# K and V of an attention kernel read as rows of two keys, two partial row sums, and a third tile in every fourth head on TensorE

## The chip, the cores and the metric

The kernel runs on one core of one Trainium2 chip. The metric is the device time of one execution in microseconds. Before the change it is 1547.74 us, the median of three runs (1547.68 to 1548.92). One more execution was taken with the hardware profiler; the views in this document are from that one.

## What is computed

A block of a transformer with adaptive normalization. The heavy part is attention of 2048 queries over a cache of 2048 keys, 32 heads of 128, in bf16:

```python
h = _layernorm(x, axis=-1) * (1 + ca) + sa
q = (h @ wq).reshape(B, Sq, 32, 128).transpose(0, 2, 1, 3)
scores = jnp.einsum('bhqd,bhkd->bhqk', q, k_cache) * 128 ** (-0.5)
p = _softmax(scores, axis=-1)
o = jnp.einsum('bhqk,bhkd->bhqd', p, v_cache)
x = x + ga * (o.transpose(0, 2, 1, 3).reshape(B, Sq, 4096) @ wo)
```

After it come a second normalization and a mixer with an MLP on the 2048 x 640 activations. The change does not touch them.

## The kernel before

Every engine has one list of instructions, written out in program order by the functions `op` and `dma`, which also work out the semaphore waits from the keys that an instruction reads and writes. Nothing reorders a list later: an instruction that waits holds up all that stands behind it on its engine. SyncE (SP) issues nearly all transfers, so its list is also the order in which they enter the DMA queue q1. GpSimd (POOL) issues the stores of the attention output into a scratch tensor in memory, `o_scratch` (line 477).

The attention loop (line 560) runs over 512 steps, 32 heads of 16 query tiles of 128 queries. In step s:

- TensorE multiplies the query tile with all 2048 keys of the head, in two halves of two 512-column matmuls each (`qk`, lines 299 and 15), into `Sps`. Between the halves and behind them stand the halves of the P V product of the step eight back (`pv`, line 313; `PVD` is 8), and the small pieces below.
- VectorE scales each half by the negative factor, writes it to `negS` in SBUF and takes the row minimum (line 606). GpSimd joins the two minima (line 611). ScalarE takes the exponential into a slot of a ring of ten, `Pb` (line 614).
- The exponentials have queries on the partitions, and P V needs keys there, so each tile is transposed. Most tiles go by DMA within SBUF (`transpose`, line 233), two neighbouring tiles in one transfer where possible. Some are done by TensorE in float32 pairs of bf16 values (`t_piece`, line 265: eight 128x128 transposes a tile, spread over two steps), and ScalarE copies them out of PSUM (`t_evac`, line 272: two copies of 512 columns a tile). `PE_STEPS` has two patterns: kind 0 gives TensorE the tiles 3 and 10 of a head, kind 1 the tiles 2, 3 and 10; each number behind a tile is the step at which its pieces begin. `kind(h)` is `h % 2`, so heads have two and three such tiles in turn.
- In the first kind the DMA transposes 14 tiles of a head in eight transfers, six pairs and two singles (tiles 2 and 11); in the second 13 tiles in seven, six pairs and a single (tile 11).
- The queries of the next head are made in 20 pieces of one 512-column matmul (`q_piece`, line 248) with four copies on ScalarE (line 255), placed where no transpose piece stands.

`pv` multiplies 16 blocks of 128 keys with `Vaug`, whose blocks have 130 columns: 128 of V and a one, so that the 129th result is the row sum of the exponentials. Two query tiles share a PSUM bank; ScalarE copies both, 259 columns, to `Of` (line 593). For every four tiles GpSimd raises the four row sums to the power of -1 (`rcp`, line 463), multiplies (`norm`, line 470) and stores.

The loads of a head come on SyncE between the transposes: at step 2 K of the next head (`load_k`, line 216, a transposing DMA of 2048 rows of 128), at step 6 the weights of the queries (`load_wq`, line 220), at step 9 V of the next head (`load_v`, line 225: 16 blocks of 128 keys, 256 bytes a key). K, V and wq have two buffers each.

The ones beside V are written once at the start: GpSimd fills a scratch area, TensorE transposes it, ScalarE copies it, GpSimd copies a part of it into `Vaug` (lines 357 to 365).

Behind the loop the kernel loads the attention output transposed from memory (`load_ot`, line 520; the first parts already within the last head) and runs the output projection (line 548) and the rest.

Of the kernel before, what the change touches and what calls it, by code (L numbers as in the profile page):

```python
# [9 lines left out]
F32 = mybir.dt.float32  # L10
# [113 lines left out]
def bass_adaLN_cond__mha_block_cached__mixer_s_mlp__prompt_kernel(  # L124
# [6 lines left out]
    KT = D // 128  # L131
# [14 lines left out]
    with ExitStack() as es:  # L146
# [9 lines left out]
        if True:  # L156
            with ExitStack() as es1:
# [3 lines left out]
                PE_STEPS = ({3: 6, 10: 13}, {2: 5, 3: 7, 10: 14})  # L161
                kind = lambda h: h % 2
                US = KT * (SQ + 4)
# [18 lines left out]
                KTs = kv[:, 0:o1].rearrange("p (b s) -> p b s", b=2)  # L182
                Vaug = kv[:, o1:o2].rearrange("p (b k d) -> p b k d", b=2, k=NKT)
                wq = kv[:, o2:o3].rearrange("p (b k d) -> p b k d", b=2, k=KT)
# [29 lines left out]
                def load_k(h):  # L214
                    hb = h % 2
                    G.dma("sync", lambda e: e.dma_start_transpose(KTs[:, hb], A_k_cache[0, h]), ("k", hb), w=[("KT", hb)])

# [5 lines left out]
                def load_v(h):  # L223
                    hb = h % 2
                    G.dma("sync", lambda e: e.dma_start(Vaug[:, hb, :, 0:128], A_v_cache[0, h].rearrange("(t p) d -> p t d", p=128)),
                          ("v", hb), w=[("V", hb)])
# [78 lines left out]
                def pv(g, half):  # L305
                    hb = (g // NQT) % 2
                    b = g % RP
                    ob = PO[:, ((g // 2) % 2) * 512 + (g % 2) * 130:]

                    def f(t):  # L310
                        for kt in range(half * 8, half * 8 + 8):
                            pt = PTr[:, b, kt // 2, :, kt % 2] if is_pe(g) else PTs[:, b, kt, :]
                            ins = t.matmul(ob[:, 0:129], pt, Vaug[:, hb, kt, 0:129],  # L313
                                           start=(kt == 0), stop=(kt == NKT - 1))
                        return ins
                    G.op("tensor", f, r=[("PT", b, half), ("V", hb), "ones"], w=[("O", (g // 2) % 2)])

# [28 lines left out]
                if H > 1:  # L346
# [9 lines left out]
                G.op("gpsimd", lambda g: g.tensor_copy(identf[:], ident), r=["ident"] + ringk(IO, IO + 128), w=["identf"])  # L356
                half1 = flat[:, 0:256].rearrange("p (q z) -> p q z", z=2)
                G.op("gpsimd", lambda g: g.memset(half1, 0.0), w=["h0", ("Pb", 0)])
                G.op("gpsimd", lambda g: g.memset(half1[:, :, 0], 1.0), r=["h0"], w=["h1"])
                G.op("tensor", lambda t: t.transpose(JB[0][:, 0:128], flat[:, 0:256].bitcast(F32), identf[:]),  # L360
                     r=["h1", "identf"], w=[("J", 0)])
                G.op("scalar", lambda a: a.copy(flat[:, 256:512].bitcast(F32), JB[0][:, 0:128]), r=[("J", 0)], w=["h2"])
                G.op("gpsimd", lambda g: g.tensor_copy(
                    Vaug[:, :, :, 128:130], flat[:, 256:384].rearrange("p (b k y z) -> p b k y z", b=2, k=NKT, z=2)[:, :, :, :, 0]),
                    r=["h2", ("Pb", 0)], w=["ones"])
                G.op("scalar", lambda a: a.activation(s_col, c_sb, ACT.Silu), r=["c"], w=["scol"])
# [94 lines left out]
                def rcp(gr):  # L461
                    b = gr % 2
                    G.op("gpsimd", lambda g: g.tensor_tensor(  # L463
                        out=rl[:, 4 * b:4 * b + 4], in0=Of[:].rearrange("p a z d -> p (a z) d")[:, 4 * b:4 * b + 4, 128],
                        in1=mone, op=ALU.pow),
                         r=[("Of", 2 * b), ("Of", 2 * b + 1), "mone"], w=[("rl", b)])

                def norm(gr, z):
                    b = gr % 2
                    G.op("gpsimd", lambda g: g.tensor_scalar(  # L470
                        out=On[:, b, z, :], in0=Of[:, 2 * b + z // 2, z % 2, 0:128],
                        scalar1=rl[:, 4 * b + z:4 * b + z + 1], scalar2=1.0, op0=ALU.mult, op1=ALU.mult),
                        r=[("Of", 2 * b + z // 2), ("rl", b)], w=[("On", b, z)])
                    if z < 3:
                        return
                    hh, jj = divmod(4 * gr, NQT)
                    G.dma("gpsimd", lambda e: e.dma_start(  # L477
                        o_scr[jj // 2:jj // 2 + 2, :, hh].rearrange("a p z d -> p a (z d)"),
                        On[:, b].rearrange("p (a z) d -> p a (z d)", a=2)),
                        ("o", b), r=[("On", b, z) for z in range(4)], w=[("os", b), ("osd", jj // 4, hh)])  # L480
# [79 lines left out]
                for s in range(NG + PVD + LAG):  # L560
# [30 lines left out]
                    if 0 <= g_ < NG and g_ % 2 == 1:  # L591
                        p = g_ // 2
                        G.op("scalar", lambda a, p=p: a.copy(  # L593
                            Of[:, p % 4].rearrange("p z d -> p (z d)")[:, 0:259], PO[:, (p % 2) * 512:(p % 2) * 512 + 259]),
                            r=[("O", p % 2)], w=[("Of", p % 4)])
# [321 lines left out]
```

## Time and profile before

| what | value |
|---|---|
| median of three runs | 1547.74 us |
| profiled execution | 1553.05 us |
| its span, first to last instruction | 1550.8 us |
| first and last start of line 606 (the attention loop) | 35.6 and 1230.0 us |
| granted TensorE clock, mean | 0.997 of full speed |
| transposing transfers ring to ring (line 233) | 240, median 7.2 us from issue to landing |
| loads of V (line 225) | 32 of 512 KB, median 4.9 us |
| loads of K (line 216) | 32, median 4.8 us |
| loads of wq (line 220) | 32 of 160 KB, median 3.2 us |
| stores to o_scratch (line 477) | 128 of 128 KB, median 5.3 us |
| packets under 512 bytes | 1136640 of 1156183 |

How to read the lines shown below: the page's busy lines give an engine's busy time, its share of the span and its instructions. In a timeline a line has the start, the time from the first start to the last end of a merged run of instructions, the engine, the line of the kernel, and the operation with output and input. In the view of waits a line names who waited for whom, with the sum in us, how often, and the longest. An instruction's duration holds its latency; where instructions overlap, the distance from start to start is what the engine needs for one. The DMA queue's time of a transfer is not in the page. It is taken from the trace's packet records: each DMA engine ends a transfer with a 4-byte packet, and the time between these packets of two neighbours on the queue is what the second one took.

### The profile page before, as it was taken

How to read it: one execution, taken by the hardware profiler on the slowest of the kernel's cores; microseconds unless marked ns; L12 is line 12 of the kernel's file. 1: busy time of each engine (PE TensorE's matmuls, PEld its weight loads, DVE VectorE, ACT ScalarE, POOL GpSimd, SP SyncE). 2: the span in 40 equal slices, each digit the busy share in tenths (PEclk: the TensorE clock that was granted, in tenths of full speed). 3: DMA queues.
4: the chain of work that ended last, by engine and by line, in shares of the span. 5: the costliest groups of instructions: out<-in, count | busy, mean ns of one | idle time of the engine just before them, and what ended most of it. 6: DMA issues, size and time to landing. Idle time of an engine off the chain costs nothing.

```text
span 1550.8 us, 32538 instructions
## 1 busy us (share of the span) xinstructions
PE 1472.3 (95%) x13447; PEld 909.8 (59%) x12664; DVE 1375.2 (89%) x2431; ACT 1259.8 (81%) x1179; POOL 625.8 (40%) x1399
## 2 busy tenths in 40 slices
PE   4899999999999999999999999999999899999999
PEld 3466656565656666666665665666665555554545
DVE  6999999999999999999999999999999747667425
ACT  4999999999999999999999999999999800034230
POOL 1144444444444444444444444444444433323100
PEclk8999999999999999999999999999999999999999
DMA  9999999999999999999999999999999999825100
GB/s 293 242 233 230 246 241 226 240 234 245 229 243 242 235 242 245 234 244 234 239 240 235 239 228 243 237 239 247 235 233 233 226 239 194 156 56 134 35 22 35
DMA packets 1156183, 330.32 MB, mean 213 GB/s; under 512 B 1136640, under 2 KB 1150016, under 8 KB 1156032
## 3 DMA queue, kind: packets, MB, share of 16 engines
q1 hardware_dynamic: 1147552, 307.10, 101.4%
q0 software_dynamic: 6144, 16.79, 3.4%
q10 hardware_dynamic: 2336, 4.34, 0.8%
q8 instruction: 104, 1.70, 0.5%
q14 instruction: 47, 0.39, 0.1%
HBM read 43.48 MB, written 19.40 MB: 41 GB/s over the span
## 4 chain that ended last, share of the span: by engine, by line
ACT 59%; PE 18%; DVE 10%; DMA 7%; issue 3%; POOL 2%; POOLq 0%; DVEq 0%
ACT ring L614 49%; DVE negS L606 8%; PE Sps L548 7%; DMA ring<-ring 5%; ACT ring L272 4%; PE Sps L854 4%; ACT Of L593 3%; ACT kv L255 3%; PE QPp L805 2%; PE Oaug L805 2%; DMA negS<-o_scratch 1%; PE Sps L790 1%; DVE ring L387 1%; POOL o_scratch L477 0%; DMA kv<-Of 0%
## 5 line engine op out<-in xcount | busy, mean ns | idle before, releaser
L606 DVE TENSOR_SCALAR_CACHE_REDUCE negS<-Sps 128x1024 f32<-128x1024 f32 x1024 | 1175.4, 1222 | 21.8 <-PE Sps L15 21.2
L614 ACT ACTIVATE ring<-negS,small 128x2048 bf16<-128x2048 f32 x512 | 1057.2, 2097 | 10.3 <-POOL small L611 9.2
L313 PEld LDWEIGHTS PTp<-kv,ring 128*128 128x128 bf16 x8192 | 554.2, 98 | 348.2 <-issue 109.1
L313 PE MATMUL PTp<-kv,ring 128*128 128x129 bf16 x8192 | 645.4, 220 | 28.3 <-DMA ring<-ring 27.0
L611 POOL TENSOR_SCALAR small<-small 128x1 f32<-128x1 f32 x512 | 147.1, 287 | 599.6 <-DVE negS L606 599.5
L15 PE MATMUL Sps<-kv 128*128 128x512 bf16 x1008 | 381.9, 379 | 5.4 <-DVE negS L606 1.7
L299 PE MATMUL Sps<-kv 128*128 128x512 bf16 x957 | 367.5, 384 | 16.3 <-DVE negS L606 5.1
L470 POOL TENSOR_SCALAR On<-Of,small 128x128 bf16<-128x128 f32 x512 | 191.7, 375 | 13.0
L299 PEld LDWEIGHTS Sps<-kv 128*128 128x128 bf16 x1024 | 98.2, 96 | 113.8 <-DVE negS L606 81.8
L463 POOL TENSOR_TENSOR small<-Of,small 128x4 f32<-128x4 f32 x128 | 133.3, 1042 | 10.2 <-ACT Of L593 10.2
L593 ACT COPY Of<-PTp 128x259 f32<-128x259 f32 x256 | 116.1, 454 | 15.0 <-PE PTp L313 15.0
L477 POOL DMA_DIRECT2D o_scratch<-On x128 | 103.4, 808 | 40.8 <-POOL On L470 37.2
L248 PE MATMUL Oaug<-hTx,kv 128*128 128x512 bf16 x257 | 97.0, 382 | 3.8 <-DVE hTx L419 3.8
L248 PE MATMUL QPp<-hTx,kv 128*128 128x512 bf16 x259 | 96.7, 378 | 3.5 <-ACT hTx L414 2.8
L735 ACT ACT_TABLE_LOAD x1 | 1.3, 1283 | 114.5 <-POOL hTx L753 114.5
L606 DVE DVE_READ_ACCUMULATOR negS<-Sps 128x1 f32 x1024 | 87.3, 85 | 0.0
L648 POOL TENSOR_SCALAR negS<-negS 128x1 f32<-128x1 f32 x48 | 24.2, 505 | 126.4 <-DVE negS L657 126.4
L548 PE MATMUL Sps<-wo,negS 128*128 128x128 bf16 (+1 forms) x503 | 69.9, 298 | 3.2 <-DMA negS<-o_scratch 2.8
L548 PE MATMUL Sps<-wo,hTx 128*128 128x512 bf16 (+1 forms) x502 | 69.3, 297 | 0.5
L858 DVE TENSOR_TENSOR ring<-Sps,ring 128x640 f32<-128x640 f32 x15 | 12.4, 824 | 59.5 <-PE Sps L854 59.5
L662 DVE TENSOR_TENSOR ring<-Sps,mod_bc 128x640 f32<-128x640 f32 x16 | 13.1, 821 | 56.0 <-PE Sps L548 33.2
L265 PE MATMUL QPp<-identf,ring 128*128 128x128 f32 x320 | 61.7, 274 | 0.0
(94 smaller groups left out, 1048.4 us busy)
## 6 DMA issues: line engine op xcount, KB each, us to landing
kv<-in_A_v_cache_dram SPq DMA_DIRECT2D x32, 512.0 KB, 4.9
o_scratch<-On POOLq DMA_DIRECT2D x128, 128.0 KB, 5.3
kv<-in_A_wq_dram SPq DMA_DIRECT2D x32, 160.0 KB, 3.2
wo<-in_A_wo_dram SPq DMA_DIRECT2D x1, 5120.0 KB, 16.9
ring<-ring SPq DMA_TRANSPOSE x240, 7.2
ring<-in_A_x_dram SPq DMA_DIRECT2D x5, 640.0 KB, 6.6
ring<-in_w_mod_dram SPq DMA_DIRECT2D x1, 3200.0 KB, 14.2
out_dram<-wo SPq DMA_DIRECT2D x15, 160.0 KB, 1.8
```

Of the source, the lines that this page charges most:

```text
L15: return t.add_instruction(mybir.InstMatmult(name=t.bass.get_next_instruction_name(), ins=[t.lower_ap(rhs), t.lower_ap(lhsT)], outs=[t.low ...
L248: G.op("tensor", lambda t: t.matmul(JB[jb], wq[:, hb, q, :], hT[:, q, cc * 512:(cc + 1) * 512], start=(q == 0), stop=(q == KT - 1)), r=[(" ...
L299: ins = (t.matmul if c2 == 0 else partial(same_weights, t))(Sps[:, col:col + 512], QT[:, hb, j * 128:(j + 1) * 128], KTs[:, hb, col:col + ...
L313: ins = t.matmul(ob[:, 0:129], pt, Vaug[:, hb, kt, 0:129], start=(kt == 0), stop=(kt == NKT - 1))
L463: G.op("gpsimd", lambda g: g.tensor_tensor(out=rl[:, 4 * b:4 * b + 4], in0=Of[:].rearrange("p a z d -> p (a z) d")[:, 4 * b:4 * b + 4, 128 ...
L470: G.op("gpsimd", lambda g: g.tensor_scalar(out=On[:, b, z, :], in0=Of[:, 2 * b + z // 2, z % 2, 0:128], scalar1=rl[:, 4 * b + z:4 * b + z ...
L477: G.dma("gpsimd", lambda e: e.dma_start(o_scr[jj // 2:jj // 2 + 2, :, hh].rearrange("a p z d -> p a (z d)"), On[:, b].rearrange("p (a z) d ...
L548: ins = t.matmul(YB[b][:, c0:c0 + cw], OTj[pr % 2][:, 2 * hh + z, :], wo[:, hh, c0:c0 + cw], start=(hh == 0), stop=(hh == H - 1))
L593: G.op("scalar", lambda a, p=p: a.copy(Of[:, p % 4].rearrange("p z d -> p (z d)")[:, 0:259], PO[:, (p % 2) * 512:(p % 2) * 512 + 259]), r= ...
L606: G.op("vector", lambda v, half=half, dst=dst, src=src, r8=r8: v.tensor_scalar(out=dst, in0=src, scalar1=-SCALE, scalar2=None, op0=ALU.mul ...
L611: G.op("gpsimd", lambda g, r8=r8: g.tensor_scalar(out=nm[:, r8:r8 + 1], in0=nm0[:, r8:r8 + 1], scalar1=nm1[:, r8:r8 + 1], scalar2=None, op ...
L614: G.op("scalar", lambda a, s=s, r8=r8: a.activation(Pb[:, s % RP, :], negS[:, s % 3, :], ACT.Exp, bias=nm[:, r8:r8 + 1], scale=-1.0), r=[( ...
```

## The change

`Vaug` holds eight rows of two keys for each partition in place of sixteen blocks of one: row t of partition p has keys 256 t + 2 p and 256 t + 2 p + 1, one behind the other, with a one ahead of the first and a one behind the second. V is read in runs of 512 bytes. The first half of P V uses the even keys, the second the odd ones; the first starts at the leading one, the second at the first column of the odd key, and writes one PSUM column further on. So the 128 output columns add up over all keys, the first column holds the row sum over the even keys and the last one that over the odd keys. K's columns get the same order by a transposing load that sees K as 1024 rows of two keys. The copy to `Of` takes 260 columns. `rcp` adds the two sums before the power. The ones are written by two fills; the transpose and the copy of the start go. `kind` gives three tiles to TensorE in every fourth head only (1, 5, 9, ...); the others have two.

```diff
-                kind = lambda h: h % 2
+                kind = lambda h: 1 if h % 4 == 1 else 0
...
-                Vaug = kv[:, o1:o2].rearrange("p (b k d) -> p b k d", b=2, k=NKT)
+                Vaug = kv[:, o1:o2].rearrange("p (b k d) -> p b k d", b=2, k=NKT // 2)
...
-                    G.dma("sync", lambda e: e.dma_start_transpose(KTs[:, hb], A_k_cache[0, h]), ("k", hb), w=[("KT", hb)])
+                    G.dma("sync", lambda e: e.dma_start_transpose(
+                        KTs[:, hb].rearrange("p (z i) -> p z i", z=2), A_k_cache[0, h].rearrange("(i z) d -> i (z d)", z=2)),
+                        ("k", hb), w=[("KT", hb)])
...
-                    G.dma("sync", lambda e: e.dma_start(Vaug[:, hb, :, 0:128], A_v_cache[0, h].rearrange("(t p) d -> p t d", p=128)),
+                    G.dma("sync", lambda e: e.dma_start(Vaug[:, hb, :, 2:258], A_v_cache[0, h].rearrange("(t p z) d -> p t (z d)", p=128, z=2)),
...
-                        for kt in range(half * 8, half * 8 + 8):
+                        for c_ in range(8):
+                            kt = half * 8 + c_
                             pt = PTr[:, b, kt // 2, :, kt % 2] if is_pe(g) else PTs[:, b, kt, :]
-                            ins = t.matmul(ob[:, 0:129], pt, Vaug[:, hb, kt, 0:129],
-                                           start=(kt == 0), stop=(kt == NKT - 1))
+                            v0 = 1 + 129 * half
+                            ins = t.matmul(ob[:, half:half + 129], pt, Vaug[:, hb, c_, v0:v0 + 129],
+                                           start=(kt == 0), stop=(kt == NKT - 1), skip_group_check=True)
...
-                half1 = flat[:, 0:256].rearrange("p (q z) -> p q z", z=2)
-                G.op("gpsimd", lambda g: g.memset(half1, 0.0), w=["h0", ("Pb", 0)])
-                G.op("gpsimd", lambda g: g.memset(half1[:, :, 0], 1.0), r=["h0"], w=["h1"])
-                G.op("tensor", lambda t: t.transpose(JB[0][:, 0:128], flat[:, 0:256].bitcast(F32), identf[:]),
-                     r=["h1", "identf"], w=[("J", 0)])
-                G.op("scalar", lambda a: a.copy(flat[:, 256:512].bitcast(F32), JB[0][:, 0:128]), r=[("J", 0)], w=["h2"])
-                G.op("gpsimd", lambda g: g.tensor_copy(
-                    Vaug[:, :, :, 128:130], flat[:, 256:384].rearrange("p (b k y z) -> p b k y z", b=2, k=NKT, z=2)[:, :, :, :, 0]),
-                    r=["h2", ("Pb", 0)], w=["ones"])
+                G.op("gpsimd", lambda g: g.memset(Vaug[:, :, :, 1:2], 1.0), w=["ones"])
+                G.op("gpsimd", lambda g: g.memset(Vaug[:, :, :, 258:259], 1.0), w=["ones1"])
...
-                    G.op("gpsimd", lambda g: g.tensor_tensor(
-                        out=rl[:, 4 * b:4 * b + 4], in0=Of[:].rearrange("p a z d -> p (a z) d")[:, 4 * b:4 * b + 4, 128],
-                        in1=mone, op=ALU.pow),
-                         r=[("Of", 2 * b), ("Of", 2 * b + 1), "mone"], w=[("rl", b)])
+                    ofs = Of[:].rearrange("p a z d -> p (a z) d")[:, 4 * b:4 * b + 4]
+                    G.op("gpsimd", lambda g: g.tensor_tensor(out=rl[:, 4 * b:4 * b + 4], in0=ofs[:, :, 0], in1=ofs[:, :, 129], op=ALU.add),
+                         r=[("Of", 2 * b), ("Of", 2 * b + 1)], w=[("rl", b)])
+                    G.op("gpsimd", lambda g: g.tensor_tensor(out=rl[:, 4 * b:4 * b + 4], in0=rl[:, 4 * b:4 * b + 4], in1=mone, op=ALU.pow),
+                         r=["mone", ("rl", b)], w=[("rl", b)])
...
-                        out=On[:, b, z, :], in0=Of[:, 2 * b + z // 2, z % 2, 0:128],
+                        out=On[:, b, z, :], in0=Of[:, 2 * b + z // 2, z % 2, 1:129],
...
-                            Of[:, p % 4].rearrange("p z d -> p (z d)")[:, 0:259], PO[:, (p % 2) * 512:(p % 2) * 512 + 259]),
+                            Of[:, p % 4].rearrange("p z d -> p (z d)"), PO[:, (p % 2) * 512:(p % 2) * 512 + 260]),
```

More of the change, by code (lines that the diff above doesn't have):

```diff
@@ L310, in f @@
                     def f(t):
-                        for kt in range(half * 8, half * 8 + 8):
+                        for c_ in range(8):
+                            kt = half * 8 + c_
                             pt = PTr[:, b, kt // 2, :, kt % 2] if is_pe(g) else PTs[:, b, kt, :]
-                            ins = t.matmul(ob[:, 0:129], pt, Vaug[:, hb, kt, 0:129],
-                                           start=(kt == 0), stop=(kt == NKT - 1))
+                            v0 = 1 + 129 * half
+                            ins = t.matmul(ob[:, half:half + 129], pt, Vaug[:, hb, c_, v0:v0 + 129],
+                                           start=(kt == 0), stop=(kt == NKT - 1), skip_group_check=True)
                         return ins
-                    G.op("tensor", f, r=[("PT", b, half), ("V", hb), "ones"], w=[("O", (g // 2) % 2)])
+                    G.op("tensor", f, r=[("PT", b, half), ("V", hb), "ones", "ones1"], w=[("O", (g // 2) % 2)])
                 ringk = lambda a, b: [k for i in range(a // SK, -(-b // SK)) for k in (
```

## The prediction

> **What bounds the kernel now.** I read the page's busy lines first, then the waits, then the SyncE, VectorE and ScalarE timelines of one head, and last the trace's DMA packet records, which I counted by time and size.
>
> ```profile
> PE 1472.3 (95%) x13447; PEld 909.8 (59%) x12664; DVE 1375.2 (89%) x2431; ACT 1259.8 (81%) x1179; POOL 625.8 (40%) x1399
> ...
> DMA  9999999999999999999999999999999999825100
> ...
> q1 hardware_dynamic: 1147552, 307.10, 101.4%
> ```
>
> Four resources are near their limit until slice 33, where the attention loop ends (VectorE's first and last L606 start at 35.6 and 1230.0 us, a loop of 1194.4 us). Which one sets the pace is read head by head. First the two engines that work a step (one query tile):
>
> ```profile
> 361.03 1.22 DVE L606 TENSOR_SCALAR_CACHE_REDUCE negS<-Sps 128x1024 f32<-128x1024 f32 x1
> ...
> 362.18 1.22 DVE L606 TENSOR_SCALAR_CACHE_REDUCE negS<-Sps 128x1024 f32<-128x1024 f32 x1
> ```
>
> ```profile
> 351.12 0.48 ACT L593 COPY Of<-PTp 128x259 f32<-128x259 f32 x1
> 351.38 2.13 ACT L614 ACTIVATE ring<-negS,small 128x2048 bf16<-128x2048 f32 x1
> 353.28 0.70 ACT L272 COPY ring<-Oaug 128x512 f32<-128x512 f32 x1
> 353.75 2.13 ACT L614 ACTIVATE ring<-negS,small 128x2048 bf16<-128x2048 f32 x1
> ```
>
> From start to start VectorE needs 1.144 us a half, so 16 x 2 x 1.144 = 36.6 us a head. ScalarE needs 1.905 an exponential, 0.26 an Of copy, 0.47 a 512-column copy. A head with two TensorE-transposed tiles costs it 16 x 1.905 + 8 x 0.26 + (4 + 4) x 0.47 = 36.3 us, one with three (two more copies) 37.2 us. Yet from head 4 (its first exponential at 190.5 us) to head 28 (1084.8) four heads take 149.05 us, where VectorE needs 146.5 and ScalarE 2 x 36.3 + 2 x 37.2 = 147.0. What ends VectorE's and TensorE's waits:
>
> ```profile
> PEld PTp L313 <- DMA ring<-ring: 59.1, 69, 2.2
> ...
> PE PTp L313 <- DMA ring<-ring: 27.0, 43, 1.7
> ...
> DVE negS L606 <- PE Sps L15: 21.2, 29, 2.2
> ```
>
> The P V product (L313) waits for a tile that the DMA transposes; the second half of the next Q K product stands behind it on TensorE, and VectorE waits for that. The transfers are late because their queue is full:
>
> ```profile
> 332.00 21.96 SPq L233 DMA_TRANSPOSE ring<-ring  x5
> 354.00 2.34 SPq L216 DMA_TRANSPOSE kv<-in_A_k_cache_dram  x1
> 356.38 5.97 SPq L233 DMA_TRANSPOSE ring<-ring  x1
> 362.40 0.58 SPq L220 DMA_DIRECT2D kv<-in_A_wq_dram  x1
> 363.02 8.95 SPq L233 DMA_TRANSPOSE ring<-ring  x2
> 372.01 0.58 SPq L225 DMA_DIRECT2D kv<-in_A_v_cache_dram  x1
> 372.64 8.43 SPq L233 DMA_TRANSPOSE ring<-ring  x2
> ```
>
> There is no gap between issues. In head 8 (two TensorE tiles) a transfer is issued 2.9 to 5.5 us after its exponential has ended, in head 11 (three) 0.0 to 1.4: the 14-tile heads build up a backlog and the 13-tile heads work it off. From the packet records I take the time between the completion packets of neighbours on this queue (mean; median; least): a pair of tiles 4.21; 4.04; 3.63. A single after a pair 2.45; 2.18; 1.82. K 2.39; 2.30; 1.82 after a single, 2.73; 2.72; 1.86 after a pair. V 2.31; 2.25; 1.97. wq 0.83. An o_scratch store adds about 0.6 to what it meets. By means two heads need 12 x 4.21 + 2.45 + 2 x 2.56 (singles behind V) + 2.39 + 2.73 + 2 x 2.31 + 2 x 0.83 + 8 x 0.6 = 74.3 us; they take 74.5. The DMA queue is the bound, with VectorE 1.3 us a pair of heads below it.
>
> **The change, part by part.** All against the profiled execution: span 1550.8 us, 1553.05 with what lies around it; the runs' median is 1547.74, so its 5.3 us of profiling cost are taken to stay, and differences are carried over to the median.
>
> *One more tile by DMA.* Heads 3, 7, ... 31 go from three TensorE tiles to two: SyncE issues 240 ring transfers before and 248 after, each new one a single (tile 2) between a pair and K. It costs the single, 2.18 by medians, and K then stands behind a single, 2.30 for 2.72: 1.76 us; by means 2.45 + 2.39 - 2.73 = 2.11. Ends: 1.81 (2048 packets at the most that a microsecond shows, 1134, with K unchanged) and 2.45. I take 2.0: 8 x 2.0 = **+16.0 us** of queue. Behind it on SyncE stand K, the next pair, wq and V; the P V product waits for the pair.
>
> *V in rows of two keys.* 2048 packets of 256 bytes a head become 1024 of 512. Now: payload 2048 / 1134 = 1.81 us, 0.50 on top. No row has 512-byte loads. At full rate a 256-byte packet takes one DMA engine 14.1 ns (16 / 1134), a 1280-byte one 51.4 ns (311 a us while wo loads); between them 512 bytes take 23.4 ns, 1024 x 23.4 / 16 = 1.50 us. What lies on top has a ramp at the start (100 to 800 packets a us) and stretches at 890 that no SBUF-sourced tile has, so I expect most of it to shrink with the count; the quickest V of now has 0.16 on top. I take 1.70, a gain of 0.61: 31 loads in the loop, **-18.9 us** of queue. Ends: 0.31 a head (all 0.50 stays) and 1.0 (the rate of the 1280-byte loads, 400 KB a us, 1.31 us); below nothing is excluded by the same bytes in fewer packets.
>
> *K as rows of two keys.* Still 2048 packets: the ring's sources are rows of 4096 or 8192 bytes and yet all their packets have 256. Each now reads half of a 512-byte row. The nearest row is L520, which reads 256-byte pieces 16 KB apart from memory and runs at 1130 packets a us: **0**, ends +0.3 and -0.3 a head.
>
> *TensorE and ScalarE.* Eight tiles less are 64 transposes of 0.112 us and 16 copies of 0.47 (7.2 and 7.5 us). This lies beside the queue, except where 13-tile heads wait for ScalarE (37.2 us) while the queue has caught up: that is the 149.05 - 148.6 = 0.45 us of four heads not in the DMA sum. Half the three-tile heads go: 0.22 x 8 = **-1.8 us**; ends 0 and -3.6.
>
> *GpSimd.* Each of 128 L463 powers gets an add of 128x4 before it. Between L611 (0.29) and what a power costs without its elements (1042 for four, 730 for one at L650, so some 0.63) I take 0.4. In that step GpSimd then has 0.29 + 0.4 + 1.04 + 0.375 = 2.1 us (2.33 at the upper end) of VectorE's 2.29: behind it stands the next L611, for which the exponential waits; its cover is the 1.2 us a step that GpSimd idles. After the loop the last L463 is on the chain of the end: **+0.4 us**.
>
> *At nothing:* Of copies of 260 for 259; the ones columns, whose old transpose and copy ended at 3.2 us while ScalarE stood until 6.7 for c; P V matmuls whose V starts at an odd element for half 0. For these, TensorE's own work is 64 x 0.2155 + 256 x 0.058 + 20 x 0.2155 + 16 x 0.112 = 34.7 us of 36.6, so 10 ns more on 128 of them is covered; none in the trace starts there, and at the 112 ns of the float32 transposes they would add 6.9 us a head, 5.0 beyond the cover.
>
> Sum: 16.0 - 18.9 + 0 - 1.8 + 0.4 = **-4.3 us**: profiled 1548.7, median **1543.4 us**.
>
> The Trainium skill, "DMA: Bandwidth & Descriptors", section "Why small descriptors are slow (HBM only)", puts about three cycles of overhead on each packet, 11 cycles for 256 bytes; by it two such packets take 22 cycles and one of 512 takes 19, an estimated 14% off V, which is less than I take. The same page's "Specifications" put the least size for line rate at 512 bytes; by that V would gain more than I take. The trace agrees with a price per packet (14.1 ns against 51.4 for five times the bytes) and shows nothing at 512.
>
> **Rivals.**
> 1. *The queue pays more than V gives back (slower).* V's 0.50 stays: 31 x 0.31 = 9.6; the singles cost their mean without a cheaper K, 8 x 2.45 = 19.6. Net +10, median **1557.7**. It decides once V gains under 0.5 us a head. For it: heads 2, 3, 0 now stand in a row with 14 tiles each and no 13-tile head between. Against: K behind a single has been the quicker one by median and by mean. The Trainium skill's "DMA: Bandwidth & Descriptors", section "Why small descriptors are slow (HBM only)", would give V about this gain.
> 2. *V at the large packets' rate (much faster).* It gains 31 x 1.0, the queue needs 148.6 + 2.0 - 4.0 = 146.6 for four heads, and VectorE's 146.5 is next: (149.05 - 146.5) x 7.75 = -19.8 at most; with bursts left some -15, median **1533**. The Trainium skill's "DMA: Bandwidth & Descriptors", section "Specifications", speaks for it with its least size for line rate. Against: V starts with a ramp that the packets' size need not shorten.
> 3. *K's half rows cost 0.3 us a load:* 30 x 0.3 = 9 on top of the forecast, **1552**. L520 speaks against it.
> 4. *The odd start doubles half of the P V matmuls:* 5 us a head, some **1700**. Nothing in the trace speaks for it.
>
> **How the numbers follow.** A measurement here can tell about 0.2%, 3.1 us: faster is under 1544.6, slower over 1550.8. Forecast 0.42, with its own range 1538 to 1548 (faster 0.29, same 0.13). Rival 1: 0.30, 1549 to 1561 (slower 0.24, same 0.06). Rival 2: 0.17, faster. Rival 3: 0.08 (slower 0.05, same 0.03). Rival 4: 0.03, slower. So faster 0.46, same 0.22, slower 0.32. The range is 1531 to 1558: rival 4, the top of rival 1 and the foot of rival 2 stay out.
>
> **What would show it.** 248 L233-like issues. V's packets 512 bytes, and 1.70 us between its neighbour's completion packets and its own (1.3: rival 2, 2.0: rival 1). K's 2.3 to 2.7 unchanged. DVE's wait for PE Sps below 21.2 us, and PTp's waits for the DMA below 59.1 and 27.0. SyncE's issues still without gaps; with gaps, rival 2. L313's matmuls still some 58 ns apart. Wrong would be: the lag behind the exponentials growing through heads 2, 3 and 0 beyond 5.5 us.

## The result and the profile after

The changed kernel is slower: median 1565.1 us of five runs (1561.56 to 1565.87) against 1547.8 us of five runs of the kernel before on the same chip (1547.68 to 1550.81), ratio 1.0087 with a 95% interval of 1.0071 to 1.0103. The ratio is an estimate from the runs on record and not the quotient of the two medians, which is 1.0112. The profiled execution took 1565.63 us, with a span of 1563.5.

The page's busy lines, the DMA line of the 40 slices and the queue q1, of the changed kernel:

```profile
PE 1482.9 (95%) x13623; PEld 891.5 (57%) x12599; DVE 1376.4 (88%) x2431; ACT 1256.5 (80%) x1161; POOL 647.3 (41%) x1526
...
DMA  9999999999999999999999999999999998725100
...
q1 hardware_dynamic: 1131424, 311.30, 98.9%
```

VectorE's work is what it was and ScalarE's is 3.3 us less, yet the attention loop (first to last start of VectorE's line, now 604) lasts from 35.4 to 1241.7 us, 11.9 us longer. The queue has 16128 packets fewer, and the time of its packets still comes to 98.9% of the 16 engines' span. The waits say where the loop lost its time:

```profile
PEld PTp L317 <- DMA ring<-ring: 84.2, 87, 2.5
...
PE PTp L317 <- DMA ring<-ring: 41.7, 61, 1.9
DVE negS L604 <- PE Sps L15: 31.8, 44, 2.2
```

These three were to fall below 59.1, 27.0 and 21.2 us; all have risen by 10 us or more. In the chain that ended last, the transfers ring to ring held 5% of the span before and now hold 18%. Before:

```profile
ACT ring L614 49%; DVE negS L606 8%; PE Sps L548 7%; DMA ring<-ring 5%; ACT ring L272 4%; PE Sps L854 4%; ACT Of L593 3%; ACT kv L255 3%; PE QPp L805 2%; PE Oaug L805 2%; DMA negS<-o_scratch 1%; PE Sps L790 1%; DVE ring L387 1%; POOL o_scratch L477 0%; DMA kv<-Of 0%
```

The changed kernel:

```profile
ACT 49%; PE 21%; DMA 20%; DVE 6%; issue 3%; POOL 1%; SPq 0%; DVEq 0%
ACT ring L612 40%; DMA ring<-ring 18%; PE Sps L546 8%; DVE negS L604 4%; PE Sps L852 4%; ACT ring L274 3%; ACT Of L591 3%; ACT kv L257 2%; PE Oaug L803 2%; PE QPp L803 2%; PE PTp L317 2%; PE Sps L788 1%; DMA negS<-o_scratch 1%; DVE ring L384 1%; PE Sps L15 1%
```

SyncE's timeline around head 12 shows a queue with no gap: each entry starts where the one before ends.

```profile
475.88 0.58 SPq L222 DMA_DIRECT2D kv<-in_A_wq_dram  x1
476.51 8.59 SPq L235 DMA_TRANSPOSE ring<-ring  x2
485.14 0.58 SPq L227 DMA_DIRECT2D kv<-in_A_v_cache_dram  x1
485.76 21.02 SPq L235 DMA_TRANSPOSE ring<-ring  x5
506.82 2.38 SPq L216 DMA_TRANSPOSE kv<-in_A_k_cache_dram  x1
```

By the trace a ring transfer is issued up to 6.9 us after its exponential has ended in head 11 and 6.6 in head 12, 6.0 in head 7 and 5.7 in head 8; in the kernel before it is at most 5.5 up to head 30. The lag is longest in the stretch between two three-tile heads: VectorE idles 1.4 to 1.8 us in each of the heads 3, 7, 11, 15, 19 and 23, where before it idled at most 0.7.

GpSimd's added sum is the first of these two groups (columns: instructions, then least, median and most ns, then the times in us from the first to the last); the power behind it is unchanged:

```profile
L461 POOL TENSOR_TENSOR small<-Of x128: 192/193/218, 70.0 to 1261.1; 128x4 f32<-128x4 f32 x128
L463 POOL TENSOR_TENSOR small<-small x128: 1035/1040/1055, 70.3 to 1261.4; 128x4 f32<-128x4 f32 x128
```

Measured between the 4-byte completion packets, V takes 2.72 us by mean in the changed kernel, where it took 2.31. The single behind V (tile 11) got quicker, 2.45 for 2.63 (loads that met a store to `o_scratch` included), so the two together take 5.17 us for 4.94. V's packets are 512 bytes, 32768 of them.

### The profile page after: what moved, and what is told of

Same layout as the page of the kernel before. It is cut to its first block, busy times and chain, and to the rows that moved or that the text cites. A ratio compares the mean times of both kernels' runs of the same rounds, so it can differ in the third digit from the quotient of the medians.

```text
span 1563.5 us, 32782 instructions
## 1 busy us (share of the span) xinstructions
PE 1482.9 (95%) x13623; PEld 891.5 (57%) x12599; DVE 1376.4 (88%) x2431; ACT 1256.5 (80%) x1161; POOL 647.3 (41%) x1526
## 3 DMA queue, kind: packets, MB, share of 16 engines
q1 hardware_dynamic: 1131424, 311.30, 98.9%
## 4 chain that ended last, share of the span: by engine, by line
ACT 49%; PE 21%; DMA 20%; DVE 6%; issue 3%; POOL 1%; SPq 0%; DVEq 0%
ACT ring L612 40%; DMA ring<-ring 18%; PE Sps L546 8%; DVE negS L604 4%; PE Sps L852 4%; ACT ring L274 3%; ACT Of L591 3%; ACT kv L257 2%; PE Oaug L803 2%; PE QPp L803 2%; PE PTp L317 2%; PE Sps L788 1%; DMA negS<-o_scratch 1%; DVE ring L384 1%; PE Sps L15 1%
## 5 line engine op out<-in xcount | busy, mean ns | idle before, releaser
L612 ACT ACTIVATE ring<-negS,small 128x2048 bf16<-128x2048 f32 x512 | 1039.6, 2047 | 20.8 <-POOL small L609 19.4
L317 PEld LDWEIGHTS PTp<-kv,ring 128*128 128x128 bf16 x8192 | 544.7, 97 | 361.7 <-issue 92.6
L317 PE MATMUL PTp<-kv,ring 128*128 128x129 bf16 x8192 | 634.7, 220 | 42.1 <-DMA ring<-ring 41.7
L301 PE MATMUL Sps<-kv 128*128 128x512 bf16 x1024 | 394.1, 385 | 11.1 <-DVE negS L604 5.5
L15 PE MATMUL Sps<-kv 128*128 128x512 bf16 x1024 | 388.0, 379 | 0.0
L463 POOL TENSOR_TENSOR small<-small 128x4 f32<-128x4 f32 x128 | 133.2, 1041 | 10.0
L250 PE MATMUL Oaug<-hTx,kv 128*128 128x512 bf16 x320 | 121.7, 385 | 4.0 <-ACT hTx L411 3.1
L250 PE MATMUL QPp<-hTx,kv 128*128 128x512 bf16 x320 | 119.8, 378 | 2.6 <-ACT hTx L411 1.9
L475 POOL DMA_DIRECT2D o_scratch<-On x128 | 103.4, 808 | 40.8 <-POOL On L468 37.2
L591 ACT COPY Of<-PTp 128x260 f32<-128x260 f32 x256 | 103.5, 404 | 14.3 <-PE PTp L317 14.3
L604 DVE DVE_READ_ACCUMULATOR negS<-Sps 128x1 f32 x1024 | 90.9, 89 | 0.0
L546 PEld LDWEIGHTS Sps<-wo,negS 128*128 128x128 bf16 x512 | 40.5, 99 | 35.7 <-DMA negS<-o_scratch 2.6
```

What stands on the lines that cost most here:

```text
L15: return t.add_instruction(mybir.InstMatmult(name=t.bass.get_next_instruction_name(), ins=[t.lower_ap(rhs), t.lower_ap(lhsT)], outs=[t.low ...
L250: G.op("tensor", lambda t: t.matmul(JB[jb], wq[:, hb, q, :], hT[:, q, cc * 512:(cc + 1) * 512], start=(q == 0), stop=(q == KT - 1)), r=[(" ...
L301: ins = (t.matmul if c2 == 0 else partial(same_weights, t))(Sps[:, col:col + 512], QT[:, hb, j * 128:(j + 1) * 128], KTs[:, hb, col:col + ...
L317: ins = t.matmul(ob[:, half:half + 129], pt, Vaug[:, hb, c_, v0:v0 + 129], start=(kt == 0), stop=(kt == NKT - 1), skip_group_check=True)
L463: G.op("gpsimd", lambda g: g.tensor_tensor(out=rl[:, 4 * b:4 * b + 4], in0=rl[:, 4 * b:4 * b + 4], in1=mone, op=ALU.pow), r=["mone", ("rl" ...
L475: G.dma("gpsimd", lambda e: e.dma_start(o_scr[jj // 2:jj // 2 + 2, :, hh].rearrange("a p z d -> p a (z d)"), On[:, b].rearrange("p (a z) d ...
```

## The experiments

Ratios are to the kernel before on the same chip, with 95% intervals. The chips differ: beside the first four kernels the kernel before had a median of 1546.74 us, beside the next four 1551.9, beside `v_none`, `wq_v`, `kb_wq_v` and `kind_more` 1553.71, beside `v_sb256`, `v_sb512` and `after_more` 1546.87, and beside the last three 1553.28. "V" and "single" are means between completion packets in one profile, some 30 loads of V each. A transposing transfer leaves two such packets on each engine; the second one counts, and the middle of the 16 engines is taken. The standard error of V's mean is 0.03 to 0.07 us, that of V plus the single behind it 0.09 to 0.16.

**The parts of the change.** `kind_back` is the changed kernel with the old pattern of TensorE tiles, `kind_only` the kernel before with the new one:

```diff
kind_back:
-                kind = lambda h: 1 if h % 4 == 1 else 0
+                kind = lambda h: h % 2
kind_only:
-                kind = lambda h: h % 2
+                kind = lambda h: 1 if h % 4 == 1 else 0
```

`v_only` has the change's diff without the lines of K and `kind` (V's load, the P V product, the two sums, the ones), `k_only` the lines of K alone.

> The changed kernel with kind(h) = h % 2 again, so that TensorE has its eight tiles back and only the order of K and V is new. Theory A (both parts charge the queue: V's load takes 2.72 us for 2.31 by the completion packets, the single behind it a little less, some 0.3 us a head): 1553 to 1558, SyncE's ring transfers back at 240, V still 2.7 us. Theory B (only the moved tiles charge it, V's longer time lies in a hole that was there anyway): 1545 to 1550. The prediction on record (V gains 0.6 us a head) would have 1530 to 1536.

> The kernel before with kind(h) = 1 in every fourth head only; K and V as before. Theory A: a single tile more in eight heads at 2.0 us of queue each is +16, less what the 13-tile heads waited for ScalarE: 1556 to 1564, below the changed kernel's 1565. Theory B: 1563 to 1567, the changed kernel's own time. The prediction on record had +14.

> The kernel before with V in rows of two keys, the two partial sums and the fills, but K in its old order and the old kind; the weights of a key so meet another key's V, which the time does not see. Theory A: V's 512-byte load alone slows the loop, 1552 to 1557, V 2.6 to 2.8 us between completion packets, with a hole at its start. If K's new rows are what slows V or the loop, 1535 to 1548 and no hole.

> The kernel before with K transposed as rows of two keys, V in its old order; the weights of a key so meet another key's V, which the time does not see. Theory A: K as before, 1545 to 1551, 2.3 us behind a single and 2.7 behind a pair. If K's half rows cost 0.3 us a load: 1555 to 1559.

Measured: `kind_back` 1.0020 (1.0004 to 1.0035), `kind_only` 1.0067 (1.0045 to 1.0088), `v_only` 1.0021 (1.0006 to 1.0036), `k_only` 1.0017 (1.0004 to 1.0030). The tiles and the rest add up to the change's 0.87%. `kind_only` came as theory A had it, at the foot of its range. `kind_back` with 1550.36 us and `v_only` with 1549.03 lie below theory A's ranges; for `kind_back` that is the top of theory B's. The waits of `kind_back` stand within 0.4 us of the kernel before:

```profile
PEld PTp L317 <- DMA ring<-ring: 59.2, 74, 2.3
...
PE PTp L317 <- DMA ring<-ring: 27.3, 37, 1.8
DVE negS L604 <- PE Sps L15: 21.6, 27, 2.2
```

and those of `kind_only` do not:

```profile
PEld PTp L313 <- DMA ring<-ring: 74.7, 83, 2.4
...
PE PTp L313 <- DMA ring<-ring: 34.5, 56, 1.8
DVE negS L606 <- PE Sps L15: 24.3, 38, 2.2
```

So the moved tiles make the kernel slower, and V's gain is missing rather than outweighed: with V in 512-byte rows and the old pattern of tiles, V plus the single behind it take 4.82 us (`v_only`) and 4.88 (`kind_back`) against 4.94. These sums can't be told apart: the other kernels that load V from memory in 256-byte rows on this queue at the same place have 4.77 to 5.05, those with 512-byte rows 4.82 to 5.17. V alone can: 2.18 to 2.31 us with 256-byte rows, 2.49 to 2.72 with 512. K costs nothing that the queue shows (in `k_only` 2.66 us behind a pair, 2.50 behind a single; before 2.73 and 2.39). Where the 0.2% of `kind_back`, `v_only` and `k_only` lies was not shown.

**Larger rows, another queue.** Is it the packet's size or something each load pays once?

```diff
v_1k: + dma_start(Vq[:, hb, :, 2:514], A_v_cache[0, h].rearrange("(t p z) d -> p t (z d)", p=128, z=4))
v_4k: + dma_start(Vf[:, hb, 0:2048], A_v_cache[0, h].rearrange("(p z) d -> p (z d)", p=128))
before_vpool, kind_back_vpool:
-     G.dma("sync", lambda e: e.dma_start(Vaug...
+     G.dma("gpsimd", lambda e: e.dma_start(Vaug...
```

> The kernel before (kind and K as before) with V in rows of four keys, 1024-byte runs with gaps between them; the 129th column is a neighbouring V column or a one, so row sums are left out. Theory C (V's load has a fixed price: its first data come from memory only some 2.5 us after the issue, the queue runs dry behind the pair ahead, and fewer packets only deepen that hole): V and the single behind it together 4.7 to 5.0 us as with 256 and 512 bytes, 1545 to 1551. Theory D (only 512-byte runs are bad, larger ones have their rate): V 1.4 to 1.6, 1533 to 1541.

> As the last, with V in rows of sixteen keys, one run of 4096 bytes a partition: 128 packets a load; the 129th column is the next block's first V column, so row sums are left out. Theory C: V and the single behind it 4.6 to 5.0 us, 1544 to 1551, and in the half microseconds before the first V packets a hole at least as deep as with 512 bytes. Theory D: V 1.3 to 1.5, 1532 to 1540.

> The kernel before, only with V's load (256-byte runs) issued by GpSimd. Theory C: 1534 to 1543, a little above the last run, since 2048 packets take 0.3 us more of the engines than 1024. Theory E: 1545 to 1551.

> The changed kernel with the old kind and with V's load issued by GpSimd on its own queue, so that the ring's transposes need not stand behind V's wait for memory. Theory C: the queue loses V's hole and V's place, SyncE's list gets gaps, ScalarE and VectorE are next: 1533 to 1541. Theory E (V's price is its bytes on the shared DMA engines, whatever the queue): 1546 to 1553. If GpSimd's issue holds up line 611: over 1553.

Measured: `v_1k` 1.0016 (1.0002 to 1.0030), V 2.80 us; `v_4k` 1.0055 (1.0036 to 1.0073), V 2.60 us and the single behind it 2.70. V and the single together take 5.13 and 5.30, more than the 4.6 to 5.0 of theory C, and theory D falls: no size of row makes V cheaper. The bytes that q1 starts, by half microsecond from V's issue (KB per us, mean of about 30 loads), show why:

```
us from issue  0    0.5  1    1.5  2    2.5  3    3.5  4    4.5
before         227  244  156  166  228  268  255  211  175  183
v_only         270  243  163  145   91  156  312  325  235  169
changed        261  269  172  125   69  125  304  332  260  162
v_1k           248  250  150   80   37  109  286  367  302  184
v_4k           252  258  191   79   87  179  283  341  229  116
v_sb256        251  243  163  214  229  221  202  187  232  187
v_sb512        220  227  160  238  257  247  229  241  205  213
```

(The last two rows are explained below.) Larger packets do run faster once data come, 304 to 332 KB a us against at most 268. But ahead of that lies a hole at 2 us, down to 69 KB a us, which the load in 256-byte packets does not have. It eats what the packets save. The engines stand without data there: from the completion ahead of V to V's own, the packets of q1 fill 109% of the 16 engines' time before (packets overlap), 81% in `v_only` and 76% in the changed kernel. A quarter of V's packets have started 0.8 us after that completion before, 1.2 in `v_only`, 1.4 in the changed kernel and 1.7 in `v_1k`.

With V issued by GpSimd the kernel before is 1.0289 (1.0240 to 1.0338) and the changed one with the old pattern 1.0492 (1.0429 to 1.0555); the gain that was hoped for there is a loss. The profile of `before_vpool` is of a run of 1614.77 us, its longest (the other three took 1590.46 to 1605.92). It has V on the other queue, 8.7 us to landing where SyncE's had 4.9. Its waits for ring transfers have a new kind of event, 12 to 13 us long, where before none was over 2.2:

```profile
PEld PTp L313 <- DMA ring<-ring: 95.9, 47, 12.9
...
DVE negS L606 <- PE Sps L15: 81.5, 40, 13.2
PE PTp L313 <- DMA ring<-ring: 73.7, 35, 12.4
```

The profile of `kind_back_vpool`, one of the shorter of its four runs, has the same events:

```profile
DVE negS L604 <- PE Sps L15: 89.5, 32, 12.5
PEld PTp L317 <- DMA ring<-ring: 88.1, 32, 12.2
```

One of them in `before_vpool`, on GpSimd's and SyncE's timelines:

```profile
215.65 1.25 POOL L225 DMA_DIRECT2D kv<-in_A_v_cache_dram  x1
```

```profile
215.49 0.58 SPq L220 DMA_DIRECT2D kv<-in_A_wq_dram  x1
216.11 28.87 SPq L233 DMA_TRANSPOSE ring<-ring  x4
```

Here four ring transfers take 28.87 us to issue, where five took 21.96 in the lines shown of before; the first of them alone takes 15.4. From 220 to 231 us q1 starts 85 to 207 packets a us in place of 1134, while V's data pass in packets of 4096 bytes on q0: 36 and 34 KB a us, where q1 alone starts 290. GpSimd itself is not late: its line 611 waits for VectorE. Why the two queues stall each other in some heads and not in all was not settled.

**Is V on the path, and can its wait be shared?** `v_none` loads V for two heads only, `wq_v` and `kb_wq_v` put the load of wq directly ahead of V.

```diff
v_none:
-                        if j == PVD + 1 and h + 1 < H:
+                        if j == PVD + 1 and h == 0:
                             load_v(h + 1)
wq_v, kb_wq_v:
-                        if j == 6 and h + 2 < H:
+                        if j == PVD + 1 and h + 2 < H:
                             load_wq(h + 2)
```

> The kernel before, in which V is loaded for heads 0 and 1 alone and these two serve all heads (30 loads of V are left out, so the output is not the reference's). Theory F, V lies on the queue that sets the pace, and its price is 2.3 us a head whatever its rows: 30 x 2.3 = 69 us of queue go, and VectorE with its 36.6 us a head is next, so the time falls by what lies between the queue's 149.05 us of four heads and VectorE's 146.5, some 15 to 20 us (ratio 0.987 to 0.990). Rival G, V's transfer is filled in by its neighbours, and what the attention loop loses lies with the ring transposes' own waits: the time falls by under 5 us (ratio above 0.997).

> The kernel before, with wq's load moved from step 6 to step 9, directly ahead of V; nothing else differs. Theory F, V's price is mainly a wait for its first data that nothing behind it on the queue covers: the two loads from memory wait together, so 0.5 us or more a head go from the queue, 8 to 15 us in all (ratio 0.990 to 0.995). Rival G, the wait is covered by the neighbours already: no change (0.998 to 1.002). Rival H, wq is hidden now and gets a wait of its own beside V, whose data then come later by wq's 0.4 us: slower by 5 to 10 us (1.003 to 1.007).

> The changed kernel with two and three TensorE tiles in turn as before, and wq's load moved directly ahead of V. Theory F: V in 512-byte packets has less work for the engines (1.73 us against 2.30 by its packets' times) and loses it to the wait for the first data; with the wait shared, the gain comes out, 15 to 20 us under the kernel before (ratio 0.987 to 0.990). Rival G: as with the old place, 1.000 to 1.003. Rival H: 1.003 to 1.008.

Measured: `v_none` 0.9894 (0.9870 to 0.9918), two heads in 73.6 us. That is ScalarE's 36.3 + 37.2, so V is on the path, as theory F had it, and ScalarE, not VectorE, is what would stop a gain there. The waits for the ring transfers are nearly gone:

```profile
PEld PTp L313 <- DMA ring<-ring: 10.6, 16, 1.8
...
DVE negS L606 <- PE Sps L15: 7.3, 5, 2.2
...
PE PTp L313 <- DMA ring<-ring: 4.8, 6, 1.7
```

`wq_v` is 1.0010 (0.9994 to 1.0025), `kb_wq_v` 1.0053 (1.0034 to 1.0073). So rival G came in the first and rival H in the second. V's own distance falls to 2.16 and 2.29 us, but the single behind it rises to 2.95 and 2.80: the wait moves on to the next transfer, and the idea that it could be shared falls.

**V without memory.** What was left open was whether the hole comes from memory or from plain packets behind transposing ones. `v_sb256` and `v_sb512` copy the other V buffer within SBUF, in the kernel before and in `v_only`:

```diff
v_sb256:
+                    if h > 1:
+                        G.dma("sync", lambda e: e.dma_start(Vaug[:, hb, :, 0:128], Vaug[:, 1 - hb, :, 0:128]),
+                              ("v", hb), r=[("V", 1 - hb)], w=[("V", hb)])
+                        return
v_sb512, in v_only:
+                        G.dma("sync", lambda e: e.dma_start(Vaug[:, hb, :, 2:258], Vaug[:, 1 - hb, :, 2:258]),
```

> The kernel before, with every load of V from head 2 on replaced by a copy of the other V buffer within SBUF, of the same 512 KB in the same 256-byte packets on the same queue at the same place (V is not read from memory there, so the output is not the reference's). Theory F, V's load begins with a wait of 0.5 to 1 us for the first data from memory, which shorter work of its packets cannot shrink: the copy has no such wait and takes what its packets need, 2048 at 1134 a us, 1.8 to 2.0 us against 2.31 from memory. Rival I, the hole comes from the change from transposing to plain packets, whatever their source: 2.2 to 2.4 us as from memory.

> The same copy within SBUF in the kernel that has V in rows of two keys and K and the TensorE tiles as before: 512-byte packets (K's order of keys does not match V's, and V is not read from memory from head 2 on). Theory F: with no wait for memory the smaller count comes out, 1.5 to 1.75 us against 2.53 from memory, 0.25 to 0.5 below the copy in 256-byte packets, and the time falls under the kernel before by 5 to 15 us (ratio 0.990 to 0.997). Rival I: 2.4 to 2.6 us, the same hole as from memory, ratio 1.000 to 1.003. Rival J, 512-byte packets are no faster a byte in this queue: as the copy in 256-byte packets within 0.1 us.

Measured: `v_sb256` 1.0011 (0.9996 to 1.0025), V 2.44 us; `v_sb512` 0.9976 (0.9959 to 0.9993), V 2.15 us by mean, 1.66 at least. The table above has no hole in either. Taken as above, from the completion ahead of V to V's own, the packets fill 99% and 100% of the engines' time, and a quarter of V's have started after 0.6 us in both. From memory the wider rows cost 0.22 us more (2.53 in `v_only` against 2.31), within SBUF they save 0.29. So the hole in the 512-byte load is memory's, about 0.4 us a head (2.53 against 2.15). The theory's sizes were too large, though: 2.15 us lies between theory F's 1.5 to 1.75 and rival I's 2.4 to 2.6, and the copy in 256-byte packets gains nothing, near its rival's 2.2 to 2.4. 0.4 to 0.6 us above the least that the packets need (1.81 us for 256 bytes at the highest rate, 1.73 for 512 by the median packet) stay without memory.

The page's DMA issues of `v_sb512` (last column: us to landing; V from memory has 5.1 in the changed kernel):

```profile
kv<-kv SPq DMA_DIRECT2D x30, 512.0 KB, 4.5
```

**How many tiles on the queue.** `kind_more` (and `kind_more_5`, the same kernel) gives TensorE three tiles in three heads of four, `kind_all` in every head, `after_more` (and `after_more_5`) is the changed kernel with the first of these.

```diff
kind_more, after_more:
-                kind = ...
+                kind = lambda h: 0 if h % 4 == 0 else 1
kind_all:
-                kind = ...
+                kind = lambda h: 1
```

> The kernel before with three TensorE tiles in three heads of four in place of two of four: eight tiles less on the DMA queue, the opposite of the change's step. Theory F, the queue sets the pace: the time falls by up to the 9.7 us that the eight tiles more had cost (0.9937), by less where ScalarE's 37.2 us of a head with three tiles is met (0.996 to 0.999). Rival G, the lag matters only where heads of two tiles stand in a row: no change or slower, 1.000 to 1.004, as ScalarE and TensorE get more to do.

> The changed kernel with three TensorE tiles in three heads of four (all but 0, 4, 8, ...). If the parts add, V's and K's 1.002 and the 0.9937 of the moved tiles give 0.995 to 0.997. If V's new load, whose single runs faster behind it, only pays where the queue has air, it falls below 0.9937. If ScalarE's 37.2 us a head with three tiles is what ends now, it stands at 0.994 as the kernel before does with these tiles.

> The kernel before with three TensorE tiles in three heads of four, once more beside the next two on one chip, since the kernel before differs by up to 0.5% from chip to chip. If eight tiles less on the queue are worth what eight tiles more cost: 0.993 to 0.996. If the 0.9937 was the chip's: 0.997 to 1.0.

> The kernel before with three TensorE tiles in every head, sixteen less on the queue than before. If the queue still paces: 0.987 to 0.991, by the price of eight tiles taken twice. If ScalarE with 37.2 us a head, 1190 in all, is met, as the loop of 1191.9 us with three heads of four shows: 0.994 to 0.998, no better than three of four.

> The changed kernel with three TensorE tiles in three heads of four, on the same chip. If the parts add, V and K in the new form cost their 0.2% here too: 0.2% above kind_more_5. If the quicker work of the 512-byte packets pays once the queue has air: below kind_more_5 by 0.2% or more.

Measured: `kind_more` 0.9937 (0.9914 to 0.9961); `after_more` on another chip 0.9988 (0.9975 to 1.0000). On one chip: `kind_more_5` 0.9948 (0.9932 to 0.9964), median 1543.07 us; `after_more_5` 0.9957 (0.9944 to 0.9971), 1544.99; `kind_all` 0.9977 (0.9963 to 0.9991), 1548.75. So the kernel before with eight tiles less on the queue beats both kernels where it was run. The new form of V and K on top of it neither gains nor costs what can be told. How much the fewer tiles gain depends on the chip: `after_more` took 1544.06 us beside a kernel before of 1546.87, where none of the three cases expected for it came, and 1544.99 as `after_more_5` beside one of 1553.28. `kind_more` ran only beside kernels before of 1553; beside one of 1547 its gain may be nearer to the 0.1% of `after_more`. Waits of `kind_more_5`:

```profile
PEld PTp L313 <- DMA ring<-ring: 24.8, 33, 1.8
```

In `kind_all` the queue is hardly late any more (TensorE's weight loads wait 8.8 us in all for ring transfers, where they waited 59.1), and VectorE now also waits for ScalarE to free `negS`:

```profile
L606 DVE TENSOR_SCALAR_CACHE_REDUCE negS<-Sps 128x1024 f32<-128x1024 f32 x1024 | 1179.9, 1220 | 17.6 <-PE Sps L15 12.7 <-ACT ring L614 4.3
L614 ACT ACTIVATE ring<-negS,small 128x2048 bf16<-128x2048 f32 x512 | 1175.4, 3039 | 2.0 <-POOL small L611 2.0
```

Most of its heads take 37.2 to 37.3 us, the 37.2 of a head with three tiles on ScalarE, as the second of the cases expected had it. Three of four heads is near where queue and ScalarE meet.

## Why the prediction was wrong

**The step that failed** is the term "V in rows of two keys", -18.9 us. Two sentences of it fell: that of the 0.50 us on top of V's payload "most" would "shrink with the count", and that a loss "is excluded by the same bytes in fewer packets". The packets did get cheaper: a 512-byte packet takes an engine 27 ns by median where two of 256 bytes take 2 x 18 = 36, a quarter less (the estimate, from rates, had 23.4 for 2 x 14.1, a sixth less). V's distance nevertheless rose, from 2.31 us to 2.53 (`v_only`), 2.55 (`kind_back`) and 2.72 (changed), and V plus the single behind it stayed where it was within the error. What lay on top did not shrink with the count: in the wider load it is time without data, 81% and 76% of the engines' time filled in place of 109%, and the copy within SBUF, which has no such hole, does get the gain in part. With 0 in place of -18.9 the prediction's own sum is 16.0 - 1.8 + 0.4 = +14.6 us, 1562.3, which lies in the measured interval (1.0071 to 1.0103 of 1547.8: 1558.8 to 1563.7). That it comes so near is partly luck: the tiles cost 10.4 us in place of 14.2, and V and K in their new form 3.1 (`kind_back`, 0.20%) in place of 0.

The Trainium skill, "DMA: Bandwidth & Descriptors", section "Why small descriptors are slow (HBM only)", holds that transfers within SBUF don't pay the price of small descriptors. In these runs the size of the rows pays within SBUF, where 512-byte rows save 0.29 us of 2.44, and not from memory, where they save nothing. The measurement decides.

Point by point:

- *One more tile by DMA*, +16.0 us of queue less 1.8 for TensorE and ScalarE, 14.2: the mechanism was right, the size high. `kind_only` cost 0.67%, 10.4 us of 1547 (7.0 to 13.6), `kind_more` and `kind_more_5` gave back 0.52 to 0.63%. The predicted 248 ring issues are there, and the lag passed the 5.5 us named as a sign of being wrong. K behind a single did not stay the quicker one in the changed kernel (2.63 us, and 2.64 behind a pair). How much of the 3.8 us that are missing is the single's own price and how much TensorE's and ScalarE's relief was not separated; in `kind_only` the queue's distances give 2.66 + 2.45 - 2.71 = 2.40 us a tile, more than the 2.0 taken, so the relief is the likelier place. (The lag of 0.0 to 1.4 us that the prediction gives for head 11 leaves out that head's first transfer, 3.7 us late; nothing rests on it.)
- *K's half rows at 0*: held within its ends; `k_only` costs 0.17%, 2.6 us (0.6 to 4.6), at the edge of what can be told.
- *GpSimd's sum at 0.4 us*: 0.193 us. It stayed covered in the loop: from 100 to 1200 us the exponentials wait 6.2 us for GpSimd in the kernel before and 6.1 in `kind_back`, which has the sum. The changed kernel's 15.3 us therefore come mainly with the late tiles and not with the sum: `kind_only`, which has no sum, has 12.0.
- *The odd start at nothing*: held. P V matmuls follow each other by 55 to 60 ns, in the half with the odd start as in the other.
- *Rival 1* was the case that came: "the queue pays more than V gives back", deciding "once V gains under 0.5 us a head". It was priced at 1557.7, since it still gave V 0.31 us a head; with none of it, 9.6 us more, it would be 1567. Its own range, 1549 to 1561, ended below the measured median. *Rival 2* is refuted twice, by V's distance and by `v_1k` and `v_4k`; its floor of -19.8 us took VectorE as next, and `v_none` shows ScalarE there. The range ended at 1558 because V's lower end was set at a gain of 0.31, by an argument about packets and not by a row.

**What stays open**: why a load from memory in 256-byte packets has no hole (2.31 us, even under the copy's 2.44 within SBUF) and one in 512-byte packets has. V plus single is 5.17 us in the changed kernel and 4.88 in `kind_back`, with the same V load; with errors of 0.14 and 0.12 that may be chance.

## What to carry to other kernels

What a transfer costs on a full queue is the distance between completions, not its packets' work: look at the bytes a microsecond starts, and ask what the part above the payload is before letting it shrink with the packet count. Never exclude a loss by an argument when no row shows the new size; keep the range open on that side. When a change pays for one move on the bound resource with an expected gain from another, price the first alone: here the tile's price was measured in both directions (+0.67% on one chip, -0.52 to -0.63% on two others, for eight tiles), and the better step was the opposite one, up to the point where ScalarE's 37.2 us a head meets the queue.

## What the runs showed of the hardware

- On this full queue wider rows from memory come later: the half microsecond at 2 us after V's issue carries 228 KB a us with 256-byte packets, 91 and 69 with 512, 37 with 1024, 87 with 4096. Within SBUF it carries 229 with 256-byte packets and 257 with 512.
- A load from memory on GpSimd's queue beside transposing transfers on SyncE's can bring the transposes from 1134 packets a us to 85 to 207 for over ten microseconds; moving V there cost this kernel 2.9%. The Trainium skill, "DMA: Bandwidth & Descriptors", section "Queues, rings and completion order", has each DMA engine go round the queues packet by packet. The trace agrees that both queues' packets interleave and shows them with about the same bytes, 36 and 34 KB a us; it also shows the two together far below the 290 of q1 alone, which sharing by turns does not account for.
- The extra GpSimd sum of 128x4 takes 193 ns, the power of 128x4 behind it 1040.
